# At most three large loads in flight: a packed-attention and gated-convolution kernel on one core

## The chip, the cores and the metric

The kernel runs on one core of one Trainium2 chip. The metric is the device time of one execution in microseconds (us). A profiled execution also has a span, from its first to its last instruction. The core has five engines with queues of their own: PE (matrix), DVE (vector), ACT (scalar), POOL and SP. SP computes nothing here: it issues every transfer between the chip's memory (DRAM) and the core's buffers, in order, on one data queue that 16 transfer engines serve.

## The reference

Attention over a small packed set of 32 rows per head, attention of the queries over that packed result, and a gated convolution with two projections. Batch is 8, heads 8, sequence 576, head size 64, model width 512.

```python
def sm_attn(qq, kk, vv):
    s = scale * np.matmul(qq, kk.transpose(0, 1, 3, 2))
    s = s - np.max(s, axis=-1, keepdims=True)
    a = np.exp(s)
    a = a / (np.sum(a, axis=-1, keepdims=True) + 1e-09)
    return np.matmul(a, vv)
p_packed = sm_attn(p, k, v)
x = sm_attn(q, p_packed, p_packed)          # heads side by side: (B, S, 512)
for k in range(5):
    gate_pre += conv_w[k][None, None, :] * xp[:, k:k + S, :]   # xp: x, 4 zero rows in front
gate = 1.0 / (1.0 + np.exp(-gate_pre))
val = x @ w_val
out = (gate * val @ w_out)
```

The weights w_val, conv_w and w_out arrive as 64-bit floats and are turned into 32-bit pairs on the chip.

## The kernel before

The work is cut by batch element b (0 to 7) and, within one, into short stages. Each stage is a Python generator, and the long table `ORDER` says in which order the generators are advanced by one step; the order of every engine's instructions is fixed by that table. `InOrder` gives each engine the order of the program. A capital letter in the table is a load: K, Q and V load k, q and v of one batch element, P the packed rows of two batch elements, L the weights. Small letters are the computing stages (a: packed attention, s and t: attention of the queries, w and v: value projection, x and g: convolution and gate, o: output projection).

The loads, all issued by `sp.dma_start`:

- `load` (line 191) brings k or q of one batch element in two pieces of 576 KB, tiles `km` and `qm`. DVE then turns each piece over into `kT` or `qT`.
- `load_v` (line 206) brings v in two pieces of 576 KB, tiles `vm`, which PE reads in the product `pv`.
- `words_of` (line 215) brings w_val and w_out in four pieces of 512 KB each (`wv_words`, `wo_words`) and conv_w in one of 20 KB (`cw_words`).
- `load_p` (line 178) brings four small pieces of 64 KB (`p`) for two batch elements.

So there are 56 large loads: 16 each of `km`, `qm` and `vm`, and 4 each of the two weights. Finished rows are written to DRAM from the tiles `osb`, by SP as well (`put`), in 36 transfers of 256 KB.

A load waits for its buffer: the numbers in `NB` say how many buffers a tile has (two for `km`, `qm` and `vm`). Besides, the framework counts landings in eight semaphores in turn, one for each transfer whatever its size, so that a transfer waits for the one eight places ahead of it in SP's order.

Of the kernel before, what the change touches and what calls it, by code (L numbers as in the profile page):

```python
# [10 lines left out]
U32 = mybir.dt.uint32  # L11
# [30 lines left out]
 'xp': 2}  # L42

PSB = {'big': 3, 'mid': 1, 'out': 1}

WHOLE = (0, 1, 2)

# [53 lines left out]
def packed_attention_gated_conv(  # L101
# [33 lines left out]
    pe, act, dve, pool, sp = (  # L135
        InOrder(tc, e) for e in (nc.tensor, nc.scalar, nc.vector, nc.gpsimd, nc.sync)
    )
# [3 lines left out]
    P = 128  # L141
# [14 lines left out]
    def tile_of(tag, shape, dt, name, pool=sb):  # L156
        return pool.tile(shape, dt, tag=tag, name=name, bufs=NB.get(tag, 3))

    def big(name):
        return ps.tile([P, 2, 512], F32, tag="big", name=name, bufs=PSB["big"])  # L160

    def one(name, tag="mid"):
        return ps.tile([P, 512], F32, tag=tag, name=name, bufs=PSB[tag])

# [10 lines left out]

    def load_p(b):
        t = tile_of("p", [P, 2, 4, D], F32, f"p_{b}")
        for e in range(G):  # L180
            for c in range(2):
                rows = (2 * e + c) * NP
                of_e = p[b : b + 2].rearrange("b (j e) n d -> e n (b j) d", e=G)[e]
                sp.dma_start(t[rows : rows + NP].rearrange("a b j d -> a (b j) d"), of_e)
        for n in range(2):
            st["p", b + n] = t[:, n]
        yield
        act.mul(t, t, scale)
        yield

    def load(b, nm, src):
        parts = st[nm, b] = []
        for n in range(2):
            m = tile_of(f"{nm}m", [P, 2, HS // NP * D], F32, f"{nm}m_{b}_{n}")
            parts.append(m)
            at = src[b].rearrange("(j e) (i m) d -> e i j (m d)", e=G, i=2 * NP)
            sp.dma_start(m, at[:, :, 2 * n : 2 * n + 2])
            yield

    def load_k(b):  # L200
        yield from load(b, "k", k)

    def load_q(b):
        yield from load(b, "q", q)

    def load_v(b):
        for g in range(G):
            m = st["v", b, g] = tile_of("vm", [TP, 4, NB6 * D], F32, f"vm_{b}_{g}")
            of_g = v[b].rearrange("(j g) (i a) d -> g i j (a d)", g=G, a=NB6)
            sp.dma_start(m, of_g[g])  # L210
            yield

    def words_of(nm, src, rows, tag="words"):
        words = tile_of(tag, [P, DM, 2], U32, f"{nm}_words", stage if tag == "words" else sb)[:rows]
        sp.dma_start(words.rearrange("a b c -> a (b c)"), src.bitcast(U32))
        return words

    def load_weights(b):  # L220
        st["words", "wv"] = {}
        for c in range(NC):
            st["words", "wv"][c] = words_of(f"wv{c}", w_val[c * P : c * P + P, :], P)
            yield
        st["words", "cw"] = words_of("cw", conv_w, NT)
        yield
        st["words", "wo"] = {}
        for c in range(NC):
            st["words", "wo"][c] = words_of(f"wo{c}", w_out[c * P : c * P + P, :], P, "late")
            yield  # L230
# [386 lines left out]
    def project(b):  # L617
# [37 lines left out]

    streams = {
        "K": load_k, "V": load_v, "Q": load_q, "P": load_p, "L": load_weights,
        "C": conv_weights, "W": value_weights, "O": out_weights,
        "k": keys, "a": attn_pack, "q": queries, "p": packed_turned, "s": attn_out, "t": weighted,
# [48 lines left out]
```

## Time and profile before

| | |
|---|---|
| time, median of 3 runs | 288.07 us (287.93 to 290.36) |
| time of the profiled execution | 288.72 us |
| its span | 286.9 us |
| busy: PE, DVE, ACT, POOL | 257.1, 236.1, 164.6, 132.3 us |
| moved by transfers | 43.56 MB |

The profiled execution took 1.8 us more than its span and lies 0.65 us above the median. A row that begins with two numbers is from a list in order of time: start and duration in us. SPq is SP's issuing of a transfer: its time there is that of the issue, not of the transfer. In a list of waits or on the chain of waits, "issue" is time in which an engine stood still and waited for nothing that the profile shows.

### The profile page before, as it was taken

How to read it: one execution, taken by the hardware profiler on the slowest of the kernel's cores; microseconds unless marked ns; L12 is line 12 of the kernel's file. 1: busy time of each engine (PE TensorE's matmuls, PEld its weight loads, DVE VectorE, ACT ScalarE, POOL GpSimd, SP SyncE). 2: the span in 40 equal slices, each digit the busy share in tenths (PEclk: the TensorE clock that was granted, in tenths of full speed). 3: DMA queues.
4: the chain of work that ended last, by engine and by line, in shares of the span. 5: the costliest groups of instructions: out<-in, count | busy, mean ns of one | idle time of the engine just before them, and what ended most of it. 6: DMA issues, size and time to landing. Idle time of an engine off the chain costs nothing.

```text
span 286.9 us, 8501 instructions
## 1 busy us (share of the span) xinstructions
PE 257.1 (90%) x3676; PEld 191.0 (67%) x3676; DVE 236.1 (82%) x313; ACT 164.6 (57%) x306; POOL 132.3 (46%) x118
## 2 busy tenths in 40 slices
PE   0545789979899999999999999999999999999994
PEld 0143456667678766777677778766886688687863
DVE  2989489859969887899999989999998999787720
ACT  3372467729863558755847675758755465752421
POOL 1544286838778772324554317254074417401520
PEclk9997559979999999999999999999999999999999
DMA  7999953956594558783620664117111111110114
GB/s 264 318 318 292 329 206 89 279 135 181 204 324 131 197 158 220 198 238 125 200 79 37 203 202 121 73 59 220 39 39 53 57 39 73 40 53 21 39 43 177
DMA packets 25839, 43.56 MB, mean 152 GB/s; under 512 B 5829, under 2 KB 11973, under 8 KB 25802
## 3 DMA queue, kind: packets, MB, share of 16 engines
q1 hardware_dynamic: 25802, 43.02, 48.5%
q8 instruction: 29, 0.48, 0.7%
q14 instruction: 8, 0.07, 0.1%
HBM read 33.57 MB, written 9.44 MB: 150 GB/s over the span
## 4 chain that ended last, share of the span: by engine, by line
PE 66%; DVE 18%; ACT 6%; issue 4%; DMA 2%; POOL 1%; SPq 1%; ACTq 0%; DVEq 0%
PE o L84 26%; PE val L84 13%; DVE sig L84 10%; PE s L84 8%; PE x L84 7%; PE pv L84 5%; PE at L84 4%; DMA wv_words<-in_moe_w_val_dram 2%; PE wp L84 2%; ACT sig L84 1%; PE ppTt L84 1%; ACT a L84 1%; SPq L84 1%; PE spread L84 1%; DVE a2l L84 1%
## 5 line engine op out<-in xcount | busy, mean ns | idle before, releaser
L84 POOL TENSOR_TENSOR gvl<-sig,gvh 128x576 fp32r<-128x576 f32 x32 | 51.3, 1604 | 64.7 <-ACT gvh L84 64.5
L84 DVE SCALAR_TENSOR_TENSOR sig<-xp,cw,sig 128x576 f32<-128x576 f32 x80 | 71.1, 888 | 3.2 <-ACT sig L84 1.8
L84 PE MATMUL o<-woh,gvh 128*128 128x512 f32 x144 | 58.9, 409 | 2.3 <-ACT osb L84 1.6
L84 PE MATMUL o<-woh,gvl 128*128 128x512 f32 x144 | 56.9, 395 | 0.0
L84 PE MATMUL o<-wol,gvh 128*128 128x512 f32 x144 | 56.7, 394 | 0.0
L84 PE MATMUL val<-a2h,wph 128*128 128x288 f32 x128 | 39.9, 312 | 0.0
L84 PE MATMUL val<-a2h,wpl 128*128 128x288 f32 x128 | 38.5, 301 | 0.0
L84 PE MATMUL val<-a2l,wph 128*128 128x288 f32 x128 | 38.2, 299 | 0.0
L84 PEld LDWEIGHTS o<-woh,gvh 128*128 128x128 f32 x144 | 27.0, 188 | 13.7 <-ACT osb L84 3.6
L84 ACT CAST gvh<-sig 128x576 fp32r<-128x576 f32 x32 | 21.6, 674 | 25.3 <-DVE sig L84 25.2
L84 DVE SCALAR_TENSOR_TENSOR sig<-sig,val 128x576 f32<-128x576 f32 x32 | 23.7, 740 | 10.5 <-PE val L84 7.0
L84 PEld LDWEIGHTS o<-woh,gvl 128*128 128x128 f32 x144 | 27.1, 188 | 6.8 <-POOL gvl L84 0.5
L84 ACT ACTIVATE osb<-o 128x512 f32<-128x512 f32 x34 | 20.3, 596 | 17.8 <-PE o L84 14.8
L84 PEld LDWEIGHTS o<-wol,gvh 128*128 128x128 f32 x144 | 27.1, 188 | 5.0
L84 POOL TENSOR_TENSOR t<-t,mx 128x576 f32<-128x576 f32 x16 | 20.1, 1254 | 21.8 <-DVE mx L84 21.8
L84 POOL TENSOR_TENSOR t<-t,rs 128x576 f32<-128x576 f32 x16 | 21.9, 1368 | 17.4 <-DVE rs L84 17.3
L84 PEld LDWEIGHTS val<-a2h,wph 128*128 128x128 f32 x128 | 24.6, 192 | 5.2 <-issue 2.0
L84 PEld LDWEIGHTS val<-a2h,wpl 128*128 128x128 f32 x128 | 24.6, 192 | 0.8 <-DVE wpl L84 0.3
L84 PEld LDWEIGHTS val<-a2l,wph 128*128 128x128 f32 x128 | 24.6, 192 | 0.0
L84 ACT ACTIVATE sig<-sig 128x576 f32<-128x576 f32 x20 | 13.7, 685 | 19.0 <-DVE sig L84 18.9
L84 PE MATMUL s<-kT,pT 32*32 32x288 f32 x512 | 16.0, 461 | 9.5 <-DVE kT L84 9.3
L84 PEld LDWEIGHTS pv<-vm,a1t 96*32 96x32 f32 x768 | 13.3, 119 | 13.9 <-issue 6.1
(80 smaller groups left out, 455.6 us busy)
## 6 DMA issues: line engine op xcount, KB each, us to landing
km<-in_k_dram SPq DMA_DIRECT2D x16, 576.0 KB, 5.9
vm<-in_v_dram SPq DMA_DIRECT2D x16, 576.0 KB, 6.9
qm<-in_q_dram SPq DMA_DIRECT2D x16, 576.0 KB, 6.8
out_dram<-osb SPq DMA_DIRECT2D x36, 256.0 KB, 2.1
wv_words<-in_moe_w_val_dram SPq DMA_DIRECT2D x4, 512.0 KB, 6.1
wo_words<-in_moe_w_out_dram SPq DMA_DIRECT2D x4, 512.0 KB, 8.3
p<-in_p_dram SPq DMA_DIRECT2D x16, 64.0 KB, 4.1
cw_words<-in_moe_conv_w_dram SPq DMA_DIRECT2D x1, 20.0 KB
```

Of the source, the lines that this page charges most:

```text
L84: made = getattr(self.engine, op)(*args, **kw)
```

## The change

`fetch` takes the place of `sp.dma_start` for the large loads. It remembers the name of each large load that it issues, and makes each wait for the landing of the large load three places in front of it in SP's order. The small loads (`p`, `cw_words`) and the stores are issued as before, and they do not count.

```diff
+AT_ONCE = 3
...
+    under_way = []
+
+    def fetch(to, of):
+        made = sp.dma_start(to, of)
+        if len(under_way) >= AT_ONCE:
+            tc.add_manual_dep(
+                made.ins,
+                under_way[-AT_ONCE],
+                mybir.DependencyInfo(mybir.DependencyClass.Sync, mybir.DependencyReason.DATA),
+                reason="loads at once",
+            )
+        under_way.append(made.ins.name)
+
...
-            sp.dma_start(m, at[:, :, 2 * n : 2 * n + 2])
+            fetch(m, at[:, :, 2 * n : 2 * n + 2])
...
-            sp.dma_start(m, of_g[g])
+            fetch(m, of_g[g])
...
-        sp.dma_start(words.rearrange("a b c -> a (b c)"), src.bitcast(U32))
+        (fetch if rows == P else sp.dma_start)(words.rearrange("a b c -> a (b c)"), src.bitcast(U32))
```

The order of the instructions is the same on all five engines; only waits of SP differ. In the rows below, DMAHW0 to DMAHW7 are the eight semaphores of landings, DVE, PE and Activation those of the engines that free a buffer. The first place is SP's queue near the start of the program: `wv` are pieces of w_val, `wo` of w_out, and `km_1_0` is the first piece of k for batch element 1. Before:

```order
L84 DMA wv1_words_94<-in_moe_w_val_dram 128x1024
L84 DMA wv2_words_111<-in_moe_w_val_dram 128x1024 [waits DMAHW0_49]
L84 DMA km_1_0_148<-in_k_dram 128x2x576 [waits DMAHW1_49,DVE_49]
L84 DMA vm_0_0_152<-in_v_dram 96x4x384 [waits DMAHW2_49]
L84 DMA wv3_words_159<-in_moe_w_val_dram 128x1024 [waits DMAHW3_49]
L84 DMA km_1_1_163<-in_k_dram 128x2x576 [waits DMAHW6_49,DMAHW4_49,DVE_49]
L84 DMA cw_words_193<-in_moe_conv_w_dram 5x1024 [waits DMAHW5_49]
L84 DMA vm_0_1_252<-in_v_dram 96x4x384
L84 DMA qm_0_0_317<-in_q_dram 128x2x576 [waits DMAHW7_49]
L84 DMA qm_0_1_324<-in_q_dram 128x2x576 [waits DMAHW0_49]
L84 DMA wo0_words_332<-in_moe_w_out_dram 128x1024 [waits DMAHW1_49]
```

With the change:

```order
L86 DMA wv1_words_94<-in_moe_w_val_dram 128x1024 [waits DMAHW0_49]
L86 DMA wv2_words_111<-in_moe_w_val_dram 128x1024 [waits DMAHW1_49]
L86 DMA km_1_0_148<-in_k_dram 128x2x576 [waits DMAHW6_49,DVE_49]
L86 DMA vm_0_0_152<-in_v_dram 96x4x384 [waits DMAHW7_49,DMAHW2_49]
L86 DMA wv3_words_159<-in_moe_w_val_dram 128x1024 [waits DMAHW3_49,DMAHW0_49]
L86 DMA km_1_1_163<-in_k_dram 128x2x576 [waits DMAHW4_49,DMAHW1_49,DVE_49]
L86 DMA cw_words_193<-in_moe_conv_w_dram 5x1024 [waits DMAHW5_49]
L86 DMA vm_0_1_252<-in_v_dram 96x4x384 [waits DMAHW2_49]
L86 DMA qm_0_0_317<-in_q_dram 128x2x576 [waits DMAHW3_49]
L86 DMA qm_0_1_324<-in_q_dram 128x2x576 [waits DMAHW4_49]
L86 DMA wo0_words_332<-in_moe_w_out_dram 128x1024 [waits DMAHW6_49]
```

No row moved. `km_1_1` now waits for the landing of `km_1_0` (DMAHW1), `vm_0_1` for that of `vm_0_0` (DMAHW2), and `wo0` for that of `vm_0_1` (DMAHW6).

The second place is SP's queue some 50 us into the program, where w_out's third piece, k for batch element 3 and the second piece of v for batch element 2 are loaded. Before:

```order
L84 DMA wo2_words_758<-in_moe_w_out_dram 128x1024 [waits DVE_49,Pool_49]
L84 DMA km_3_0_778<-in_k_dram 128x2x576 [waits DMAHW7_49,DMAHW2_49,DVE_49]
L84 DMA km_3_1_797<-in_k_dram 128x2x576 [waits DMAHW3_49,DMAHW0_49,DVE_49]
L84 DMA vm_2_1_931<-in_v_dram 96x4x384 [waits DMAHW1_49,PE_49]
L84 DMA p_4_1008<-in_p_dram 32x8x64 [waits DVE_49,Activation_49]
```

With the change:

```order
L86 DMA wo2_words_758<-in_moe_w_out_dram 128x1024 [waits DMAHW3_49,DVE_49,Pool_49]
L86 DMA km_3_0_778<-in_k_dram 128x2x576 [waits DMAHW4_49,DVE_49]
L86 DMA km_3_1_797<-in_k_dram 128x2x576 [waits DMAHW5_49,DVE_49]
L86 DMA vm_2_1_931<-in_v_dram 96x4x384 [waits DMAHW6_49,PE_49]
L86 DMA p_4_1008<-in_p_dram 32x8x64 [waits DVE_49,Activation_49]
```

Again no row moved; `vm_2_1` now waits for the landing of `wo2` (DMAHW6), the third large load in front of it.

## The prediction

> **What bounds the kernel now.** I read the page first, then the chain of waits.
>
> ```profile
> PE 257.1 (90%) x3676; PEld 191.0 (67%) x3676; DVE 236.1 (82%) x313; ACT 164.6 (57%) x306; POOL 132.3 (46%) x118
> q8 instruction: 29, 0.48, 0.7%
> PE 66%; DVE 18%; ACT 6%; issue 4%; DMA 2%; POOL 1%; SPq 1%; ACTq 0%; DVEq 0%
> ```
>
> PE holds 66% of the chain, and transfers themselves only 2%: data that lands somewhat later costs little, as long as it isn't the data next read. "Issue" has 4%, 10 us or so, in which an engine stood still for nothing shown. From the chain in order of time, its three longest such pieces and what follows the last:
>
> ```profile
> 23.66 2.03 issue
> ...
> 33.77 1.52 issue
> ...
> 57.44 1.69 issue
> 59.13 1.04 PE pv L84 x43
> 60.17 3.12 PE val L84 x12
> ...
> 64.04 1.78 PE val L84 x12
> ```
>
> PE stops in mid-group (the pv products of 59.13 go on where they had stopped), so no data is missing. What is missing is code. The page's queue q8 carries only instructions: 0.48 MB in 29 transfers, and PE's 3676 products and 3676 weight loads make 7352/29 = 254 instructions for each. The counts of the stretches between these stops agree (columns: PE, PEld, DVE, ACT, POOL busy, granted clock, share of the transfer engines, GB/s):
>
> ```profile
> 0.00:23.60 23.60, 9.30 (x221) 5.11 (x222) 16.27 (x25) 11.54 (x20) 8.09 (x13) 1.00 0.94 309
> 25.60:33.60 8.00, 5.89 (x127) 3.69 (x126) 3.91 (x6) 3.61 (x9) 1.43 (x3) 0.50 1.02 262
> 35.20:57.30 22.10, 20.74 (x507) 13.63 (x507) 19.09 (x29) 15.45 (x32) 17.84 (x15) 0.83 0.64 198
> 51.62:57.30 5.68, 5.68 (x153) 3.96 (x121) 4.60 (x8) 4.09 (x10) 5.34 (x6) 1.00 1.05 308
> 59.10:66.52 7.42, 7.39 (x127) 6.71 (x127) 4.53 (x7) 3.56 (x7) 3.62 (x4) 0.77 0.56 153
> 59.70:63.10 3.40, 3.40 (x31) 3.13 (x19) 0.76 (x2) 1.15 (x3) 1.71 (x2) 0.50 0.47 113
> ```
>
> 126 loads and 127 products are one block, 507 and 507 are four. Each stop falls at the end of a block, and around each the transfer engines are near 100% busy (0.94, 1.02 and 1.05 of their time). The next two rows are the instruction queue's part of the transfers between 56.4 and 56.6 us, and between 67.1 and 67.3 us:
>
> ```profile
> q8 instruction: 1, 0.02, 39.2%
> ...
> q8 instruction: 1, 0.02, 37.0%
> ```
>
> PE began the last block before the stop at about 51.6 us (121 loads up to 57.30), yet the next block's transfer started only at 56.5: 4.9 us later, and behind several loads. The block after that stop ended at 66.5 (127 and 127 from 59.1 on), and a transfer of code started by 67.2, 0.7 us later, when the loads in front had landed and no other packet moved. So code waits behind queued data.
>
> **Part 1, the new waits: do loads land later?** First the issue times before (SP in order of time), then issue size and time to landing, from the transfers view in short windows around 9.3, 10.8, 11.7, 13.1, 27.9, 29.6, 47.9, 50.8 and 60.2 us:
>
> ```profile
> 9.27 0.38 SPq L84 DMA_DIRECT2D km<-in_k_dram  x1
> ...
> 10.79 0.38 SPq L84 DMA_DIRECT2D km<-in_k_dram  x1
> ...
> 11.66 0.34 SPq L84 DMA_DIRECT2D vm<-in_v_dram  x1
> ...
> 13.12 0.81 SPq L84 DMA_DIRECT2D wo_words<-in_moe_w_out_dram  x1
> ...
> 27.20 1.11 SPq L84 DMA_DIRECT2D qm<-in_q_dram  x2
> ...
> 29.61 0.47 SPq L84 DMA_DIRECT2D wo_words<-in_moe_w_out_dram  x1
> ...
> 47.83 0.34 SPq L84 DMA_DIRECT2D wo_words<-in_moe_w_out_dram  x1
> ...
> 50.79 0.42 SPq L84 DMA_DIRECT2D vm<-in_v_dram  x1
> ```
>
> ```profile
> km<-in_k_dram SPq DMA_DIRECT2D x1, 576.0 KB, 3.8
> ...
> km<-in_k_dram SPq DMA_DIRECT2D x1, 576.0 KB, 7.6
> ...
> vm<-in_v_dram SPq DMA_DIRECT2D x1, 576.0 KB, 9.4
> ...
> wo_words<-in_moe_w_out_dram SPq DMA_DIRECT2D x1, 512.0 KB, 14.7
> ...
> qm<-in_q_dram SPq DMA_DIRECT2D x1, 576.0 KB, 8.5
> ...
> wo_words<-in_moe_w_out_dram SPq DMA_DIRECT2D x1, 512.0 KB, 10.9
> ...
> wo_words<-in_moe_w_out_dram SPq DMA_DIRECT2D x1, 512.0 KB, 4.1
> ...
> vm<-in_v_dram SPq DMA_DIRECT2D x1, 576.0 KB, 8.1
> ...
> vm<-in_v_dram SPq DMA_DIRECT2D x1, 576.0 KB, 4.9
> ```
>
> A load with little in front of it lands in 3.8 (km), 4.1 (wo) or 4.9 us (vm); the long times are queueing. I push each new wait through. The km of 10.79 (`km_1_1`) landed at 18.4; it must now wait for the km of 9.27, landed at 13.1, and with 3.8 us could land at 16.9, still before 18.4, so it stays where the queue in front of it puts it. The vm of 11.66 landed at 21.1. wo0 (13.12) landed at 27.8; now it goes at 21.1, could land at 25.2, and stays at 27.8. wo1 (29.61) landed at 40.5; it waits for the second qm, issued at 27.9, landed at 36.4, and with 4.1 lands at 40.5: no margin, the tightest of all. The vm of 50.79 waits for wo2, landed at 47.83 + 4.1 = 51.9, and with 4.9 could land at 56.8, against 58.9 before. Behind a waiting load SP's later rows queue: the four small `p` loads behind wo0 are issued only after 21.1, but they land behind wo0 either way, and later on it is loads and stores of `osb`. Of SP's own waits these come first:
>
> ```profile
> SPq L84 <- ACT osb L84: 145.0, 28, 10.7
> ```
>
> It stands 145 us of 287 before stores whose tile ACT has yet to write, so a wait of a few us before a load is mostly taken out of that; if that cover were gone, a store kept back by 2.7 us (about two loads) would hold one of two `osb` buffers so much longer. That three in flight do fill the queue is seen where only three were there (6 to 9.5 us), against about six (33 to 38):
>
> ```profile
> 6.00:9.50 3.50, 0.21 (x8) 0.21 (x16) 2.30 (x4) 0.63 (x1) 2.32 (x2) 1.00 1.04 407
> 33.00:38.00 5.00, 3.29 (x92) 2.67 (x81) 4.39 (x8) 1.99 (x4) 3.27 (x3) 0.50 1.03 402
> ```
>
> 407 against 402 GB/s. Term 1: **0 us**; bounds 0 and, if every third load loses the tight case's slack and 1.3 us more, the slower rival below. The extra semaphores cost SP alone, which mostly waits.
>
> **Part 2, less data in front of code.** Before, the block of 56.5 had the rest of wo2, two km and at least part of the vm of 50.79 (landed at 58.9) in front of it. With the change that vm is issued at 51.9, after the block is due (51.6). A vm's own transfer takes 4.9 - 2.4 = 2.5 us (of a lone load's time some 2.4 us, 3.8 less 576 KB at 407 GB/s, pass before its data flows). So the block starts 0 to 2.5 us earlier; I take 2, nearer the upper end, since it started 2.4 us before that vm landed, when by the same split most of the vm's data must have passed. It was late by 1.69 us, so that stop goes. The other two stops: near 19 us three loads are queued now in place of four (wo0 is not yet issued), still more than that block, through by 25.69, had to wait for; near 25 us what stands in front (wo0, `p`, one vm) was held back by buffers and SP's order, not by depth, and stays. I take both as unchanged. Term 2: **-1.69 us**; bounds 0 and all three stops, -5.24.
>
> **Part 3, the clock.** After the 57.44 stop the granted clock is 0.50 for 3.4 us, and twelve val products take 3.12 us in place of 1.78, 1.34 more. Without the stop this dip should go too. From 25.6 to 33.6 the clock was 0.50 as well; at the same ratio, 1.78/3.12, the 5.89 us of PE work there would shrink by 2.5. Whether a dip falls there in other executions one profile can't show: I count the clock at 0, bounds 0 and -3.9. What is late next is DVE:
>
> ```profile
> 63.32 0.75 DVE L84 SCALAR_TENSOR_TENSOR sig<-sig,val 128x576 f32<-128x576 f32 x1 [2.83 <-PE val L84]
> ```
>
> DVE waited 2.83 us for those products, so up to that much the gain passes on, and behind it PE leads the chain again (66% of it).
>
> **The sum.** On the profiled execution 288.72 - 1.69 = 287.0; scaled to the median, which lies 0.65 lower, **286.4 us** (-0.6%).
>
> The Trainium skill bears on this twice. "DMA: Bandwidth & Descriptors", section Queues, rings and completion order, says that each transfer engine takes turns between queue rows packet by packet. By that rule a code block waits for a packet, not for loads, and the change is worth nothing; the trace disagrees with its 4.9 against 0.7 us. The same page, Rules for kernel authors, says to issue a transfer early and wait late; the change does the opposite, and by that rule it loses whenever the queue runs dry, which by the 407 GB/s it doesn't.
>
> **The rivals.**
> *Nothing moves.* A code block gets past everything but a fixed number of packets, so three loads in flight hold it as long as six. For it: the block that ended the first stop was there by 25.69, though wo0, issued at 13.12, landed only at 27.8, so code does get past data. Against: the 0.7 us of 67.2. Time: 288.1.
> *More than one stop goes.* All three (-5.24), and with both clock dips (-1.34, -2.5) at most -9.1; the likely part, two stops and a dip, is -4.5 to -5: 283.3. For it: stops and dips stand side by side. Against: part 2's count of what is in front.
> *Slower: the queue runs dry.* Place: `km_1_1` and the q after it.
>
> ```profile
> 18.37 1.33 DVE L84 STREAM_TRANSPOSE kT<-km 128x1152 f32<-128x1152 f32 x1
> ...
> 43.98 1.37 DVE L84 STREAM_TRANSPOSE kT<-km 128x1152 f32<-128x1152 f32 x1
> ```
>
> DVE turns that km over at 18.37, as it lands, so a delay there goes straight to PE. When a landing frees the third place, two loads of about 1.4 us are ahead, and a lone load needs 2.4 us before its own data flows. It decides from 2.8: if under load it were 4.1, every third load loses 1.3 us, twice to the q loads, some 2.6 to 3 us in all, for 291. Later landings have slack (that k for the next batch is read only at 43.98, over 4 us after landing).
>
> **Chances.** Forecast, 285.2 to 287.3: 0.40. Nothing moves, 287.3 to 289.2: 0.23. More than one stop, under 285.2: 0.29. Slower, from 289.2 on: 0.08, of which 0.07 above 291. The range 282.9 to 289.3 leaves out 0.1 of the larger gain and most of the slower case. A measurement of this kernel can tell about 1% from no change; by that bound, 285.2 and 291.0, faster is 0.29, same 0.40 + 0.23 + 0.01 = 0.64 and slower 0.07.
>
> **What would show it.** "Issue" after 57 us gone from the chain and no 0.50 near 60 us; landings of the first 20 loads as before within 0.5 us; SP waiting for transfers where it waited for nothing. It is wrong if the stop at 57 stays though that vm is issued at 52, if `km_1_1` lands after 19, or if the first stops go as well.

## The result, and the profile after

| | before | with the change |
|---|---|---|
| median of 20 runs each, on one chip | 287.81 us (286.01 to 290.36) | 285.29 us (283.55 to 288.69) |
| ratio of the times, with its 95% interval | | 0.9917 [0.989, 0.9944] |
| the profiled execution, and its span | 288.72 us, 286.9 us | 285.65 us, 283.9 us |

The change takes off 0.83%, or 287.81 x 0.0083 = 2.4 us (1.6 to 3.2 by the interval). The forecast was 0.6%. The gain is real, but it is under the 1% that the prediction took as the least that counts as faster. The ratio leaves out the executions that took over 1.5% more than the fastest of their kernel, so it isn't quite the quotient of the medians.

From the page of the changed kernel, the busy times, the chain's shares, and the group of DVE that multiplies the gate by the value (its last figures are DVE's idle time ahead of it, and how much of that was ended by PE's `val`):

```profile
PE 253.4 (89%) x3676; PEld 188.4 (66%) x3676; DVE 236.0 (83%) x313; ACT 164.4 (58%) x306; POOL 132.7 (47%) x118
PE 60%; DVE 20%; DMA 8%; ACT 5%; issue 3%; POOL 1%; SPq 1%; ACTq 0%; DVEq 0%
L86 DVE SCALAR_TENSOR_TENSOR sig<-sig,val 128x576 f32<-128x576 f32 x32 | 23.7, 740 | 7.6 <-PE val L86 4.1
```

The same group on the page before:

```profile
L84 DVE SCALAR_TENSOR_TENSOR sig<-sig,val 128x576 f32<-128x576 f32 x32 | 23.7, 740 | 10.5 <-PE val L84 7.0
```

DVE does the same work (236.0 for 236.1 us), and PE is busy 3.7 us less (253.4 for 257.1), though it issues the same 3676 products. Its products take longer where the granted clock is at 0.50 (twelve `val` products took 3.12 us there and 1.78 us elsewhere), and over the first 66 us the mean granted clock is 0.92 in the changed kernel's profile and 0.84 in the one before. Before, DVE stood idle 10.5 us ahead of the group shown, 7.0 of them for `val`; the 2.9 us less are about the one wait of 2.83 us that the prediction quoted. Next, the chain of waits of the changed kernel from 15 to 66 us, start and duration:

```profile
30.28 4.41 issue
34.70 1.70 PE spread L86 x51
...
51.27 1.57 PE s L86 x59
...
54.74 0.75 DVE sig L86
```

Of three stops one is left on the chain, and it is longer than any before: 4.41 us at 30.28. The stop at 57.44 is gone (PE still stood 0.61 us at 23.82, off the chain), and where the chain ran through PE's `pv` and `val` at 59 and 60 us it now runs through DVE. PE reaches the product after the long stop at 34.70, where it was 35.28 before, and the `s` of 51.27 at nearly the old time. A row of the same chain before:

```profile
51.36 1.57 PE s L84 x59
```

So in these two executions almost nothing has been won by 51 us, and the 3.0 us of span are won between 51 and 66 us. The view by stretches of the changed kernel, with the columns of the prediction's table, shows how (busy time and count of PE, PEld, DVE, ACT and POOL, the granted clock, the share of the transfer engines, GB/s):

```profile
25.60:33.60 8.00, 3.12 (x100) 1.92 (x100) 6.56 (x10) 4.53 (x10) 3.88 (x5) 0.94 1.01 237
51.62:57.30 5.68, 5.68 (x166) 3.99 (x138) 4.30 (x7) 4.01 (x10) 5.14 (x5) 1.00 0.88 241
59.70:63.10 3.40, 3.10 (x65) 2.80 (x68) 3.37 (x5) 2.89 (x6) 2.54 (x3) 1.00 1.00 296
```

From 51.62 to 57.30 PE issues 166 + 138 = 304 instructions in place of 274, straight past the end of the code block. From 59.70 to 63.10 the clock is 1.00 in place of 0.50, and PE does 65 products in place of 31 (the clock there is taken up again under term 3). The first row shows the clock at 0.94 there in place of 0.50, which bought little: PE came to the missing block 3.5 us sooner (30.28 for 33.77) and went on only 0.6 us sooner.

### The profile page after: what moved, and what is told of

Its sections match the earlier page's. It is cut to its first block, busy times and chain, and to the rows that moved or that the text cites. A ratio compares the mean times of both kernels' runs of the same rounds, so it can differ in the third digit from the quotient of the medians.

```text
span 283.9 us, 8502 instructions
## 1 busy us (share of the span) xinstructions
PE 253.4 (89%) x3676; PEld 188.4 (66%) x3676; DVE 236.0 (83%) x313; ACT 164.4 (58%) x306; POOL 132.7 (47%) x118
## 4 chain that ended last, share of the span: by engine, by line
PE 60%; DVE 20%; DMA 8%; ACT 5%; issue 3%; POOL 1%; SPq 1%; ACTq 0%; DVEq 0%
PE o L86 26%; PE val L86 12%; DVE sig L86 11%; PE x L86 7%; PE s L86 5%; DMA vm<-in_v_dram 4%; PE pv L86 3%; PE at L86 3%; DMA wo_words<-in_moe_w_out_dram 2%; PE wp L86 2%; DMA p<-in_p_dram 1%; DVE kT L86 1%; ACT sig L86 1%; DVE mx L86 1%; DVE t L86 1%
## 5 line engine op out<-in xcount | busy, mean ns | idle before, releaser
L86 PE MATMUL val<-a2h,wph 128*128 128x288 f32 x128 | 39.3, 307 | 0.0
L86 PE MATMUL val<-a2h,wpl 128*128 128x288 f32 x128 | 37.9, 296 | 0.0
L86 ACT CAST gvh<-sig 128x576 fp32r<-128x576 f32 x32 | 21.5, 673 | 22.6 <-DVE sig L86 22.6
L86 POOL TENSOR_TENSOR t<-t,rs 128x576 f32<-128x576 f32 x16 | 21.9, 1368 | 14.5 <-DVE rs L86 14.4
L86 PEld LDWEIGHTS val<-a2h,wph 128*128 128x128 f32 x128 | 24.0, 188 | 5.1 <-issue 1.8
L86 ACT ACTIVATE sig<-sig 128x576 f32<-128x576 f32 x20 | 13.7, 686 | 19.0 <-DVE sig L86 18.9
L86 DVE STREAM_TRANSPOSE qT<-qm 128x1152 f32<-128x1152 f32 x16 | 21.7, 1360 | 0.0
```

The costliest lines, as they stand in the source:

```text
L86: made = getattr(self.engine, op)(*args, **kw)
```

## Experiments

Each kernel ran beside the kernel before on the same chip. The diffs are against the changed kernel. The kernels e4 and e6 ran six times, the others ten or twelve. Large loads are counted from 0; number 24 is the `vm` that was issued at 50.79 us, number 13 the first piece of v for batch element 1 (`vm_1_0`), number 11 the second piece of q for batch element 0.

| kernel | what waits | ratio to before, 95% interval | median, before beside it |
|---|---|---|---|
| e1_only_one | only load 24 | 0.9972 [0.9941, 1.0004] | 286.13, 287.23 us |
| e2_all_but_one | all but load 24 | 0.994 [0.9901, 0.9978] | 286.38, 287.23 us |
| e3_cap2 | two in flight | 1.0072 [1.004, 1.0104] | 288.9, 287.23 us |
| e4_vm10_behind_wo0 | load 13 for load 12 in place of load 10 | 0.9888 [0.9841, 0.9934] | 284.54, 287.23 us |
| e5_three_later | loads 11 and 13 later | 0.9912 [0.9884, 0.994] | 284.41, 286.93 us |
| e6_three_later_then_two | the same, then two in flight | 0.9877 [0.9843, 0.9912] | 283.61, 286.93 us |
| e7_cap5 | five in flight | 0.999 [0.9967, 1.0014] | 286.74, 286.93 us |
| e8_late_only | only loads 21 and later | 0.9961 [0.993, 0.9992] | 285.42, 286.93 us |
| e9_early_only | only loads up to 20 | 0.9959 [0.9928, 0.999] | 285.61, 287.81 us |
| e10_cap4 | four in flight | 1.0002 [0.9966, 1.0039] | 287.45, 287.81 us |
| e11_same_again | the change itself | 0.992 [0.9889, 0.995] | 285.19, 287.81 us |
| e12_vm10_then_two | e4, then two in flight | 0.9912 [0.9879, 0.9944] | 284.89, 287.81 us |

### The load that the prediction named, alone and left out

```diff
-        if len(under_way) >= AT_ONCE:
+        if len(under_way) == 24:
```

> Of the 53 added waits only one is kept: vm_2_1 waits for the landing of wo2 (51.3 us with the change), all other loads go as before. Theory (code waits behind data that is queued when it is asked for): this one wait moves that vm behind the code block that PE needs at 57 us, so the stop of 1.69 us there goes and with it the clock dip after it; nearly the whole gain of the change, 0.989 to 0.994 of the time before. The stops at 23.7 and 33.8 stay at 2.0 and 1.5 us. Rival 1 (what counts is that fewer loads are in flight throughout): one wait of 53 gives little, 0.998 to 1.000. Rival 2 (the clock falls otherwise by chance): the stop near 57 stays.

```diff
-        if len(under_way) >= AT_ONCE:
+        if len(under_way) >= AT_ONCE and len(under_way) != 24:
```

> The change without that one wait: vm_2_1 is issued as soon as its buffer is free, all other loads wait as in the change. Theory: the stop near 57 us is back with 1.5 to 1.9 us, and what the other waits bring at the first stop (2.03 to 0.83) is lost at the second, whose block comes when it came before; 0.997 to 1.000 of the time before. Rival 1: the gain of the change is kept, 0.990 to 0.994.

With load 24 alone waiting, the stop at 57 stayed. SP in order of time, and the chain, of that kernel:

```profile
50.93 0.33 SPq L86 DMA_DIRECT2D vm<-in_v_dram  x1
```

```profile
57.61 1.55 issue
```

At first this seemed to sink the cause that the prediction gave. But the `vm` was issued at 50.93, as early as before (50.79): wo2, for which it waits, had landed at 50.85 (51.25 in the profile of the change), so the wait held next to nothing back. All the other waits without this one gave 0.994, and the stop there was 0.55 us long; the `vm` went at 48.33 there and PE began the block at 50.2, 1.5 us sooner than before. So one wait is not the whole gain, and this pair can't say more.

### Early and late waits apart

```diff
-        if len(under_way) >= AT_ONCE:
+        if len(under_way) >= 21:
```

> The change from the 22nd large load on (wo2 near 48 us), the 21 before as before. Theory: the first two stops are as before (2.0 and 1.5 us), the one near 57 us is shorter or gone; half or more of the gain, 0.993 to 0.997. If all of the gain comes from the first 45 us: 0.998 to 1.001; if all of it from later: 0.990 to 0.993.

```diff
-        if len(under_way) >= AT_ONCE:
+        if AT_ONCE <= len(under_way) < 21:
```

> Only the first 21 large loads (up to km_2_1 and wo1, issued before 50 us) keep the bound of three; the later ones go as before. The late half alone gave 0.9961. Theory 'code behind loads, both stretches': the early and late parts add up, so this gives about 0.996 (0.993 to 0.998), with the stop at 57 us back at 1.2 to 2 us and the first stop under 1.2 us. Rival 'the early gain is given back at the second stop': 0.999 to 1.001, first stop shorter and second longer by the same amount, as in the one profile of the change.

> The change itself again, for comparison on the same chip as the two halves and the bound of four. Both theories: 0.992 (0.989 to 0.995). If the profile differs from the first one in the stops near 24 and 30 us, then how the gain is split between the stops varies from one execution to the next; if it doesn't, the long stop at 30 us belongs to this version.

The halves give 0.9961 and 0.9959; their product, 0.992, is what the whole gave twice (0.9917 and 0.992). So the late waits are worth 286.93 x 0.0039 = 1.1 us, and the early ones, which the prediction had at nothing, 287.81 x 0.0041 = 1.2 us; either interval ends some 0.2 or 0.3 us from nothing. The issue times of SP and the stops on the chain say which half does what. First the late waits alone:

```profile
51.44 0.33 SPq L86 DMA_DIRECT2D vm<-in_v_dram  x1
```

```profile
24.58 1.20 issue
...
33.43 1.53 issue
```

then the early waits alone:

```profile
48.12 0.46 SPq L86 DMA_DIRECT2D vm<-in_v_dram  x1
```

```profile
24.04 0.33 issue
...
31.19 2.90 issue
...
56.49 1.92 issue
```

and the change again:

```profile
51.84 0.33 SPq L86 DMA_DIRECT2D vm<-in_v_dram  x1
```

```profile
24.08 0.33 issue
...
31.81 2.58 issue
```

The late waits remove the third stop and leave the first two (1.20 and 1.53; with load 24 alone, where no early load waits either, 1.14 and 2.36). The length of the first stop misleads by itself: with no early wait it is 2.03, 1.20 and 1.14 us in three profiles, but in all three PE goes on at 25.7 to 25.8 us. The early waits leave the third stop, shorten the first and lengthen the second in three profiles (the two above and the first of the change), and there PE goes on at 24.4. But the kernel with all waits except load 24's has the same early waits, and its profile differs. Its stops on the chain:

```profile
24.70 0.91 issue
...
32.91 0.76 issue
```

Its wo0 on SP, and then that of the change:

```profile
21.40 0.35 SPq L86 DMA_DIRECT2D wo_words<-in_moe_w_out_dram  x1
```

```profile
21.69 0.35 SPq L86 DMA_DIRECT2D wo_words<-in_moe_w_out_dram  x1
```

There PE goes on at 25.6 after the first stop, as without the waits, and both stops are under 1 us. So the early waits don't always work by the same stop. Net, PE is past the second stop at 34.7, 34.4, 34.1 and 33.7 us in the four profiles with these waits (the last is all but load 24), against 35.3, 35.0 and 35.0 in the three with none: 0.3 to 1.6 us won, which agrees with the 1.2 us timed. The rival, that the second stop takes back all that the first gave, isn't borne out, though the interval of the early half ends just where that rival begins (0.999).

### How many in flight

```diff
-AT_ONCE = 3
+AT_ONCE = 2
```

> At most two large loads in flight in place of three. Theory: vm_1_0 now goes at about 26 us, after the second block of code is asked for (24), so the second stop (4.4 us with the change) falls to 1 or 2 us; but two loads leave the queue dry, since one load of 1.4 us doesn't cover the 2.4 us before the next one's data flows: km_1_1 and the two q of batch element 0 land 1 to 3 us later and PE waits for them. Sum between 0.985 and 1.000 of the time before; the rate from 15 to 35 us under 270 GB/s. Rival 1 (fewer is better throughout): clearly faster than the change, under 0.985. Slower rival (queue dry): over 1.005.

The same line with 5 and with 4:

> At most five large loads in flight. Theory: blocks find three to five loads in front of them as before and wait 2.5 to 4.5 us; the stops at 24, 33 and 57 us are all there: 0.996 to 1.001 of the time before. Rival (it is the order in which landings are counted, or SP's waits, and not the depth): the gain of the change, 0.990 to 0.994.

> Four large loads in flight in place of three. Depth theory: the time lies between that of three (0.992) and five (0.999), about 0.995. Rival 'any bound that binds does it' (the order of landings matters, not the depth): 0.992 as with three.

Four and five are worth nothing that can be told from no change, and two is slower by 0.7%. The stretch from 9.5 to 22 us (last column GB/s), of before, of the change and of two in flight:

```profile
9.50:22.00 12.50, 7.49 (x168) 4.04 (x156) 11.19 (x17) 8.34 (x16) 5.04 (x4) 1.00 0.99 304
```

```profile
9.50:22.00 12.50, 7.56 (x168) 4.24 (x169) 11.20 (x16) 8.04 (x16) 5.03 (x4) 1.00 0.98 298
```

```profile
9.50:22.00 12.50, 6.10 (x128) 3.21 (x128) 9.38 (x14) 5.42 (x10) 4.71 (x4) 1.00 0.78 247
```

Three keep the transfer engines as busy as before (0.98 of 0.99); two leave them at 0.78, and DVE waits for k, for the piece `km_1_1` and later for the one of batch element 2. From the timeline of DVE with two in flight (in brackets its idle time and what ended it):

```profile
21.67 1.38 DVE L86 STREAM_TRANSPOSE kT<-km 128x1152 f32<-128x1152 f32 x1 [1.48 <-DMA km<-in_k_dram]
...
46.12 1.38 DVE L86 STREAM_TRANSPOSE kT<-km 128x1152 f32<-128x1152 f32 x1 [1.12 <-DMA km<-in_k_dram]
```

With two all three stops are gone (no "issue" over 0.1 us is on the chain from 18 to 66 us); the dry queue costs more than that gives. With four the late `vm` goes out at 50.46, and the stop is there. SP's timeline and the chain with four in flight:

```profile
50.46 0.42 SPq L86 DMA_DIRECT2D vm<-in_v_dram  x1
```

```profile
57.22 1.16 issue
```

### The second stop taken away

```diff
-                under_way[-AT_ONCE],
+                under_way[-1 if len(under_way) == 13 else -AT_ONCE],
```

> The change with one more wait: vm_1_0 goes only when wo0, the load just in front of it, has landed (27.6 us), the rest as in the change. Theory: vm_1_0 and vm_1_1 then stand behind the code block asked for at 24 us, which starts by 29 in place of 32.2, and the second stop of 4.4 us falls to 0.5 to 1.5 us. vm_1_0 is read at 38.2 and lands by 33, so no data is late. 0.978 to 0.985 of the time before. Rival (the block comes at 32 whatever is queued, because PE asks for it late): the stop stays at 4 us and the time at 0.99.

```diff
+LATER = (11,)
...
-                under_way[-AT_ONCE],
+                st["turned", 0] if len(under_way) == 13 else under_way[-2 if len(under_way) in LATER else -AT_ONCE],
...
-        act.copy(ppT, pt[:, : 3 * P].rearrange("a (n x) -> a n x", n=3))
+        st["turned", b] = act.copy(ppT, pt[:, : 3 * P].rearrange("a (n x) -> a n x", n=3)).ins.name
```

Here load 11 waits two places in front, and load 13 for ACT's copy into `ppT` of batch element 0, so that it goes out at 27.41 us in the profile.

> The change with two loads held longer: the second piece of q of batch element 0 waits for the load two places in front, and vm_1_0 waits until ACT has copied ppT of batch element 0 (27 to 29 us), some 1 us after PE asks for the code block it needs at the second stop. Theory (a block waits for what is in flight when PE is about 200 instructions ahead of needing it): that block starts within 1 us of being asked for (28.5 in place of 31.6 to 32.8) and the second stop goes; the first shrinks to under 1 us. vm_1_0 lands near 34, read near 37. 0.978 to 0.986 of the time before. Rival (the block's start is set by something else, since with vm_1_0 held to 27.6 it still came at 31.6): stop of 1.3 to 4 us stays, 0.988 to 0.992.

The same with `LATER = (11, *range(22, 56))`:

> As the run before, and from wo2 (48 us) on at most two loads in flight. Theory: the blocks asked for at 52, 70 and 75 us wait under 1 us, as with two in flight throughout, and no stop is left near 57, 73 and 78 us; the data has slack there: 0.976 to 0.984. Slower rival (the queue runs dry there too): k or q comes late, a wait of DVE or PE for a transfer shows between 50 and 90 us, 0.990 or more.

```diff
+BEHIND = {13: 1, **{n: 2 for n in range(22, 56)}}
...
-                under_way[-AT_ONCE],
+                under_way[-BEHIND.get(len(under_way), AT_ONCE)],
```

> The change, with the first piece of v for batch element 1 waiting for the weight piece right in front of it, and two in flight in place of three from the 23rd large load on. Depth theory: it takes both improvements of the earlier versions (0.9888 and 0.9877), so 0.985 to 0.989, with no stop over 1 us after 40 us. Rival 'the queue runs dry with two': as slow as three or slower, 0.992 to 0.997, later transposes of k starting over 1 us later.

In the change, SP issues two `vm` from 24.99 on; the first takes 6.3 us and lands at 31.3, and the missing code starts between 32.1 and 32.3. The issue in order of time, its time to landing, and the instruction queue's part of the transfers:

```profile
24.99 1.17 SPq L86 DMA_DIRECT2D vm<-in_v_dram  x2
```

```profile
vm<-in_v_dram SPq DMA_DIRECT2D x1, 576.0 KB, 6.3
...
q8 instruction: 1, 0.02, 39.2%
```

In the last kernel (e12) the first `vm` goes at 28.15, and the code's transfer lies between 28.1 and 28.3, ahead of its data:

```profile
28.15 1.42 SPq L87 DMA_DIRECT2D vm<-in_v_dram  x2
```

```profile
q8 instruction: 1, 0.02, 32.1%
```

So the block comes 4 us sooner, and the long stop goes. In e4, where only this load is moved, it goes at 27.6, the code at 31.6, and the stops are 1.58 and 0.97 us. Up to load 21 the two kernels have the same waits, so this difference is one between executions: in e4 wo0 went out at 21.13 and PE got past the first stop at 25.8, in e12 at 22.30 and 25.0. What PE waits for from 22 to 60 us, in the change (us in total, times, longest):

```profile
PE spread L86 <- issue: 4.4, 1, 4.4
...
PE pv L86 <- ACT a1t L86: 0.9, 1, 0.9
```

and in e12:

```profile
PE pv L87 <- ACT t L87: 2.7, 1, 2.7
```

A wait of 2.7 us for the tile `t` on ACT (in e5, too, 2.5 us) has taken the place of the stop and of the 0.9 us for `a1t`. That takes back part of the 4.4 us. It isn't all: in its profile e12 begins the block that the change began at 51.6 at 49.5 us, 2.1 us sooner. Yet e12 took 284.89 us where the change took 285.19 on the same chip, and the ratios 0.9912 and 0.992 can't be told apart. The profiled execution of e12 (283.78 us) lies 1.1 us under its median, so part of its lead is that one execution's; where the rest goes stays open. The lowest ratio of all, 0.9877, has an interval that overlaps the change's as well. None of these versions is shown to be better than the change.

## Why the prediction was right, and where it was not

**The bound and the cause.** That missing code stops PE is shown. In the 14 profiles PE stands over 0.25 us with "issue" as the cause 32 times between 10 and 280 us. All 32 fall at the same five places in PE's count of products and weight loads (443, 696, 1204, 1710 and 2727, whole multiples of some 254 apart), and PE goes on 2.3 to 3.2 us after a transfer of the instruction queue began, each time. That the loads in front decide how late this transfer comes is shown in the main: the stops come and go with the issue times of loads. That one load decides is read from the nine profiles below; no run moved the `vm` of 50.79 alone far enough.

**Term 2, the third stop.** Right, by the load that it named. The `vm` was forecast to go at 51.9 and went at 51.31, when wo2 had landed. SP's timeline of the changed kernel:

```profile
47.35 0.34 SPq L86 DMA_DIRECT2D wo_words<-in_moe_w_out_dram  x1
47.79 1.55 SPq L86 DMA_DIRECT2D km<-in_k_dram  x2
51.31 0.33 SPq L86 DMA_DIRECT2D vm<-in_v_dram  x1
```

The time of that `vm` to landing, and the instruction queue's part between 53.3 and 53.5 us:

```profile
vm<-in_v_dram SPq DMA_DIRECT2D x1, 576.0 KB, 6.6
...
q8 instruction: 1, 0.02, 29.2%
```

The code starts at 53.4 and not at 56.5, 1.8 us after PE began the last block in place of 4.9, while the `vm` lands only at 57.9: the code has gone past it. Two details were off. The start was 3.1 us earlier, over the bound of 2.5, because the two `km` in front came earlier as well. And the argument "issued after the block is due" isn't met: 51.31 lies 0.3 us ahead of 51.6. It still held, and the profiles in which PE begins that block between 50.7 and 51.8 us show from where: with the `vm` issued at 48.12, 50.4, 50.46, 50.79 and 50.93 (early waits, five, four, before, load 24 alone) the stop on the chain is 1.92, 0.88, 1.16, 1.69 and 1.55 us; with it issued at 51.31, 51.44 and 51.84 (the change, late waits, the change again) and at 51.27 (e4) there is none. In e4 PE still stood 0.33 us there, off the chain. The timed worth of the late waits is 1.1 us, under the 1.69 of the term, but its interval (0.2 to 2.0) holds it.

**The first two stops, "unchanged".** This step failed. The prediction had named "if the first stops go as well" as a sign of being wrong, and the first of them left the chain. I counted three loads in place of four in front of the first block and took that for no difference. But the fourth, wo0, then went out at 21.69 and no longer ahead of the code: the instruction queue's transfer lies between 23.0 and 23.2 us before and between 21.85 and 22.05 with the change. These are the rows of the two windows, before and after:

```profile
q8 instruction: 1, 0.02, 34.2%
```

```profile
q8 instruction: 1, 0.02, 34.8%
```

That is some 1.1 us sooner, and PE goes on at 24.4 in place of 25.7. It holds in four of the six profiles that have the change's waits up to there, those in which wo0 went out at 21.69 to 22.30 (the code at 21.9 to 22.6); in the other two, all but load 24 and e4, it went out at 21.40 and 21.13, ahead of the code, which came at 23.0 and 23.1 as before. In the change the second stop grew instead, since the two `vm` of 24.99 still lie in front of its block and PE came there sooner. The net is timed as the early half's 1.2 us (0.3 to 2.1), where the prediction had nothing. By these point values one part of the sum was 0.6 us too large and one 1.2 us too small. That the two came out at 0.83% where 0.6% was forecast is partly luck.

**Term 1, landings.** Nothing was lost on the path, but the landings did move, by more than the 0.5 us that I allowed: `km_1_1`, issued at 13.79, took 5.1 us and landed at 18.9 (18.4 before), and wo1, called the tightest, went out at 37.29, took 5.2 us and landed at 42.5 (40.5 before). Both had slack. DVE turns over two pieces from 18.49 on (18.37 before), so the one that it takes at 18.4 is `km_1_0`, and `km_1_1` is read some 1.3 us later: my row for "as it lands" was the wrong piece. In the kernel with two in flight `km_1_1` is the one that DVE waited for at 21.67. wo1 came 2 us late and wo2, behind it, was still issued earlier than before (47.35 for 47.83).

**SP's cover.** SP's waits in the changed kernel (us in total, times, longest):

```profile
SPq L86 <- ACT osb L86: 144.2, 28, 10.7
SPq L86 <- DMA vm<-in_v_dram: 11.9, 5, 3.3
...
SPq L86 <- DMA km<-in_k_dram: 10.9, 7, 2.4
...
SPq L86 <- PE pv L86: 7.6, 4, 4.4
...
SPq L86 <- DMA qm<-in_q_dram: 5.8, 5, 2.0
```

and the same view before:

```profile
SPq L84 <- PE pv L84: 23.0, 5, 9.1
...
SPq L84 <- DMA qm<-in_q_dram: 5.7, 3, 4.0
...
SPq L84 <- DMA vm<-in_v_dram: 1.8, 2, 1.0
...
SPq L84 <- DMA km<-in_k_dram: 0.8, 1, 0.8
```

SP now waits 11.9 + 10.9 + 5.8 = 28.6 us for landings of `vm`, `km` and `qm`, where it was 8.3. It was paid from waits for buffers rather than, as I wrote, from the wait for `osb`, which stayed (144.2 for 145.0): the wait for `pv` fell from 23.0 to 7.6 us.

**Term 3, the clock.** The prediction tied the dip at 59.7 us to the stop ahead of it, and this step failed. In the profile of load 24 alone the stop of 1.55 us is there, and the clock behind it is 1.00:

```profile
59.70:63.10 3.40, 3.40 (x47) 3.07 (x36) 2.19 (x4) 1.73 (x4) 1.89 (x2) 1.00 0.54 137
```

It is 1.00 there, too, behind the stops of the early waits (1.92 us), of four (1.16) and of five (0.88). Of the 14 profiles only the one before has that dip. So, as far as these profiles show, it belongs to that one execution and not to the change: of the 3.0 us of span between the two profiles, PE had won 2.0 at the end of the third stop and 1.2 behind it, where the dip had been. The kernel of load 24 alone, which holds next to nothing back, has a span 1.5 us under the one before (285.4 for 286.9) by the same dip. Counting the clock at nothing was right for the time: in eleven executions of the change on one chip the mean granted clock was 0.956 to 1.000, and the one at 1.000 took 285.17 us, one at 0.957 took 285.15.

**The rivals.** "Nothing moves" is out (the interval ends at 0.9944). "More than one stop goes" was right that the first stop also moves, and wrong on the size, since the second stop took part of it back. "The queue runs dry" is not what three in flight do, but it is what two do, at the place that I gave and with DVE waiting 1.48 us for it.

The Trainium skill, "DMA: Bandwidth & Descriptors", section Queues, rings and completion order, has each transfer engine take turns between queue rows packet by packet; the runs don't fit it, since code began up to 3 us sooner where a load had been issued 0.5 us later. The page "Runtime: NRT & Kernel Launch" of the Trainium skill, section Instruction fetch mechanics, gives 256 instructions for a block, with which the 254 counted here agree, and calls the crossing of a block mostly hidden, with which the 4.41 us at 30.28 do not.

What stays open: in the two profiles compared at the start, the change has won 0.6 us after the second stop and 0.1 us at 51 us, while the early half by itself is timed at 1.2 us. One execution per kernel, with dips of the clock in other places each time, can't show where the early gain is kept.

## What to carry to other kernels

When an engine stands still and the profile names no cause, count its instructions between such stops: here a constant count of some 254, and its multiples, meant code, and then what matters is which loads were issued just ahead of the request. Holding a load back until PE has asked for its code can remove a stop, but the depth has to be found by trial, with the transfer rate beside it: here five and four gave nothing, three 0.8%, and two lost 0.7%. A stop that is removed is worth only the time until the next wait: a stop of 4.4 us gave way to 2.7 us of waiting for ACT. And two profiles that differ by 3 us need a third: a kernel whose added wait held nothing back was 1.5 us shorter than the one before by a dip of the clock alone.

## What was not expected of the hardware

Between two issue times of one load that lie 0.38 us apart (50.93 in load 24 alone, 51.31 in the change), the start of a code block of 0.48 MB / 29 = 17 KB moved from 56.4 to 53.4 us. Loads on SP's queue delay code, though not as if both stood in one line: the code of 53.4 went past the `vm` issued at 51.31, which landed at 57.9. The step isn't as sharp between all profiles either: with the `vm` at 50.42 (five in flight) the code began at 54.8, and with it at 51.27 (e4) at 55.0. By contrast, the step in depth is sharp: three large loads in flight gave 0.8%, four nothing (1.0002, with an interval from 0.9966), while the rate fell off only below three (298 GB/s against 304 before, with two 247).
